# Which queue issues the loads and stores of the plain blocks, and five smaller moves, in an attention and two-layer kernel

## The chip, the core and the metric

The kernel runs on one core of a Trainium2 chip. The metric is the device time of one execution, in microseconds (us). PE is TensorE, DVE is VectorE, ACT is ScalarE, POOL is GpSimd, and SP is SyncE, which here does nothing but issue DMAs. DMAs can be issued from ACT too; each of the two has a queue of its own in the profile.

## What is computed

```python
# q, k, v: 8 x 8 x 576 x 64 (batch, heads, sequence, head width)
# attention inside chunks of 64 tokens:
scores = scale * matmul(q_c, k_c.T)
scores = scores - max(scores); attn = exp(scores); attn = attn / (sum(attn) + 1e-09)
x = matmul(attn, v_c), laid out as 4608 tokens x 512
# layer 1 (512 -> 1536 -> 512)
g = x @ w_gate; silu = g / (1 + exp(-g))
x = (silu * (x @ w_val)) @ w_out
# layer 2: the same on rows normed to unit mean square
xn = x / sqrt(mean(x * x) + 1e-6) * rms_g
out = (silu(xn @ w_gate2) * (xn @ w_val2)) @ w_out2
```

All is float32. The kernel splits each operand of a product into a high and a low half and runs three matmuls for each product (`mm3`, L642 to L645): high by high, low by high, high by low.

## The kernel before

The 4608 tokens are 36 tiles of 128 tokens. `home` (L321) gives the order in which they are worked on. The first 20 positions are five **plain blocks** of 512 tokens (`blocks`, j = 0 to 4), the list `last` (L320) names the 16 tiles behind them.

The plain blocks come first, up to about 614 us, in 60 iterations n, one for each block j and slice f of 128 columns of the 1536 (`NF` = 12). An iteration is 12 matmuls for g, 12 for v and 12 for y of the slice before, 36 in all. A list of steps (`put`, L806) is hung on it: after g, v and y of iteration n the steps 3n, 3n+1 and 3n+2 are run (`run`, in the main loop). In these steps the attention of the tiles 8 to 35 is done, one tile in about 4.5 steps: loads of q, k and v pieces (xq, xk, xv, issued through `issue`, L452), transposes on DVE (`trans_att`, L467 and L468), scores, softmax, the product with v (`att_pv`, whose result goes by `att_hi` into x of the block, or for the tail tiles through one x1 tile to memory, L607 to L613). The low halves of layer 1's weights are loaded from memory for every slice but a few, in `load_lo` (l, 512 KB) and `load_lo_o` (lo, 256 KB). Layer 2's weights are prepared beside this: loaded as w64, rebuilt, summed and stored as wsg or wsv in `comb_keep`. Layer 1's are summed for the later blocks by POOL (`whole`, L269 to L274, tiles wag, wav, wao of one tag with three buffers) and stored by SP.

Both queues issue in the order of the program. Up to iteration 19 SP issues all of it. From iteration 20 on ACT issues l and lo, right after its share of g; the stores of wsg and wsv (`comb_keep`) and the loads of w64 from the fourth on go to ACT over the whole of it. ACT also does casts (L242, L617, L675), the exponentials (L508) and the activations (L655), in one order with its issues.

Behind the plain blocks seven **large blocks** s = 0 to 6 follow, in seven products instead of eight (sums and differences of quarters). s = 0 and 1 are layer 1 of the 16 tail tiles; s = 2, 3, 4 (twice 512 tokens) and 5, 6 (twice 384) are layer 2. A large block has 84 steps for g and v (6 fp of 14 z), each of 6 matmuls at a spacing of 0.227 us (1.36 us a step), and then the y stage. Quarters of x (xf) are loaded in `x_load`, subtracted and split in `x_prep` (`sub` L1023 to L1027, `split`): for s = 0 by the table `XFIRST` in the last iterations of the plain blocks, later by `XNEXT` in the y stage. The norm of the large block before is done in the steps `extra`: sums of squares (`tail_sq`), cast and split (`tail_cast`, `tail_split`), a product with ones (`tail_mm`), root, multiply and store. In layer 2 the results are transposed into yo (`y_out`, L1204, two buffers per name) and stored by SP from a list, two or so at a time (`flush`, L1307); `rows` (L324) cuts the 512 or 384 tokens into runs that are consecutive in the output, and each run needs stores of its own.

The weights of the large blocks come through a ring of buffers (`load_ring`, L961 to L967), loaded by SP; those issues wait for the product that frees a buffer.

Of the kernel before, what the change touches and what calls it, by code (L numbers as in the profile page):

```python
# [9 lines left out]
F32 = mybir.dt.float32  # L10
# [9 lines left out]
def tile_kernel(  # L20
# [19 lines left out]
    nc = tc.nc  # L40
    B, H, S, D = q.shape
    NT, DM = out.shape
    DFF = moe_w_gate.shape[1]
    P = 128
# [205 lines left out]
    def comb_keep(nm, fp, k):  # L250
        z = SLOT[k]
        w = comb[1, nm, fp]["w", z // 2]
        a = z - z % 2
        queue = nc.sync if (nm, fp) in later2 else nc.scalar
        queue.dma_start(
            out=w2_d["gvo".index(nm), fp, :, a:z + 1], in_=w[:, :z - a + 1].bitcast(F32)
        )

    COMB = (
        (7, comb_add, 3), (7, comb_add, 4), (8, comb_add, 5), (8, comb_cast, 3), (8, comb_cast, 4),  # L260
        (9, comb_rest, 3), (9, comb_rest, 4), (11, comb_keep, 4), (10, comb_add, 6),
        (10, comb_cast, 0), (10, comb_cast, 5), (11, comb_rest, 0), (11, comb_rest, 5), (13, comb_keep, 5),
        (14, comb_cast, 1), (14, comb_cast, 6), (15, comb_rest, 1), (15, comb_rest, 6), (17, comb_keep, 6),
        (16, comb_cast, 2), (17, comb_rest, 2), (19, comb_keep, 2),
    )

    PLAIN = {"g": ((0, 0), (0, 1), (1, 1)), "v": ((0, 0), (0, 1), (1, 1)), "o": ((0, 0), (1, 0), (1, 1))}

    def whole(nm, j, p, side):  # L269
        f = 2 * p + side  # L270
        t = cv.tile([P, KD * P], F32, tag="wa", bufs=3, name=f"wa{nm}{f}")
        h = whi[0, nm, f]
        nc.gpsimd.tensor_add(t, h.bitcast(F32), low_of(0, j, chunk(j, f), nm).bitcast(F32))
        flat[0, nm, f] = t  # L274
# [42 lines left out]

    NCH = NT // CH
    SC = S // CH
    last = [12, 13, 14, 15, 20, 21, 22, 23, 28, 29, 30, 31, 32, 33, 34, 35]  # L320
    home = [i for i in range(NT // P) if i not in last] + last  # L321
    order = [home.index(i) for i in range(NT // P)]

# [283 lines left out]
    def att_hi(i, j):  # L607
        xb = xps[i]
        if j >= NB:
            t = att.tile([P, KD, P], F32, tag="x1", bufs=1, name=f"x1_{i}")  # L610
            nc.scalar.copy(t.rearrange("p h (c q) -> p c h q", c=2), xb)
            o = order[i] * P - TAIL
            nc.sync.dma_start(out=x1_d[:, o:o + P].rearrange("(h p) t -> p h t", p=P), in_=t)  # L613
            return
        xh, xl = x_tiles(0, j)
        o = order[i] * P - blocks[j][0]
        nc.scalar.copy(xh[:, :, o:o + P].rearrange("p h (c q) -> p c h q", c=2), xb)  # L617
# [270 lines left out]
    for x, (nm, f) in enumerate(w2):  # L888
        pos = NP + 8 * x
        if x == 0:  # L890
            put(0, 0, pos + 1, lambda nm=nm, f=f: load_w64(1, nm, f))
        put(0, 0, pos + 5, lambda nm=nm, f=f: rebase(1, nm, f))
        if x < 3:
            put(0, 0, pos + 8, lambda x=x: load_w64(1, *w2[x + 1]))
        elif x + 1 < len(w2):
            put(0, 0, pos + 6, lambda x=x: load_w64(1, *w2[x + 1], queue=nc.scalar))
        put(0, 0, pos + 7, lambda nm=nm, f=f: to_f32(1, nm, f))
        if f >= NP2:
            for d, fn, kk in COMB:
                put(0, 0, pos + 1 + d, lambda fn=fn, nm=nm, f=f, kk=kk: fn(nm, f - NP2, kk))  # L900

    for n in range(NF - 2, 20):
        if n >= NF:
            put(0, 0, 3 * n + 1, lambda n=n: load_lo_o(*iters[n], nc.sync))
        put(0, 0, 3 * n + 2, lambda n=n: load_lo(*iters[n + 2], nc.sync))

    w1_at = (
# [98 lines left out]
    def x_prep(s, kt):  # L1006
        tw = SB[s][1]

        def tiles(k):
            if (s, k) not in xo:  # L1010
                xo[s, k] = [
                    X2.tile(
                        [P, 1024 + (16 if (k, z) == (2, "l") else 0)], F32R, tag=f"xo{k}{z}", name=f"xo{k}{z}_{s}"
                    )[:, :1024].rearrange("p (a b) -> p a b", a=2)
                    for z in "hl"
                ]
            return xo[s, k]

        def split(k, nm):
            h, l = tiles(k)  # L1020
            x = xf[s, kt, nm]
            nc.scalar.copy(h[:, kt, :tw], x[:, :tw])
            nc.vector.tensor_sub(l[:, kt, :tw], x[:, :tw], h[:, kt, :tw].bitcast(F32))  # L1023

        def sub(o, a, b):
            o, a, b = (xf[s, kt, z][:, :tw] for z in (o, a, b))
            (nc.vector if s else nc.gpsimd).tensor_sub(o, a, b)  # L1027

        return {
            "0": lambda: split(0, "11"),  # L1030
            "A": lambda: sub("11", "12", "11"),
            "6": lambda: split(6, "22"),
            "B": lambda: sub("12", "22", "12"),
            "1": lambda: split(1, "21"),
            "C": lambda: sub("22", "22", "11"),
            "3": lambda: split(3, "11"),
            "D": lambda: sub("21", "21", "22"),
            "5": lambda: split(5, "12"),
            "4": lambda: split(4, "22"),
            "2": lambda: split(2, "21"),  # L1040
        }
# [345 lines left out]
    with tc.manual_schedule():  # L1387
# [22 lines left out]
        def conv1(z):  # L1410
# [67 lines left out]
        X2 = None  # L1478
        xops = {}
        XFIRST = {  # L1480
# [4 lines left out]
        }  # L1485
        XNEXT = {
# [6 lines left out]
        for n, (l, j, f) in enumerate(iters):  # L1493
# [31 lines left out]
            if prev is not None:  # L1525
                lo()
            sg, product = emit_g(l, j, f)
            if n >= 20 and n + 2 < len(iters):
                load_lo(*iters[n + 2], nc.scalar)
            if n >= 20:  # L1530
                load_lo_o(*iters[n], nc.scalar)
            run(0)
            if head:
                conv1(3 * f + 4 if f else 2)
# [45 lines left out]
        for s in range(NS):  # L1580
            norm = extra[s + 1]
            for z in range(2):
                for d in range(KD):
                    when(norm, 2 * d + 20 * z, tail_sq, s, z, d)
                when(norm, 8 + 20 * z, tail_cast, s, z)
                when(norm, 10 + 20 * z, tail_split, s, z)
                when(norm, 18 + 14 * z, tail_mm, s, z)
                when(norm, 34, tail_sqrt, s, z)
                when(norm, 36 + z, tail_mul, s, z)
                when(norm, 38 + 2 * z, tail_newton, s, z)  # L1590
            for n, (z, d) in enumerate(((0, 2), (0, 3), (1, 0), (1, 1), (0, 0), (0, 1), (1, 2), (1, 3))):
                when(norm, 42 + 2 * n, tail_x, s, z, d)
                when(norm, 44 + 2 * n, tail_keep, s, z, d)
        for s in range(len(SB)):
            for fp in range(NP2):
                banks = {}
                for z, (m, kk) in enumerate(GV):
                    gv_mm(s, fp, m, kk, banks)
                    wn += 1
                    if (s, fp, z) == (0, 0, 1):  # L1600
                        emit_y(*prev)
                        evac_y(*prev[:2])
                        one.close()
                        pairs.close()
                        psc = two.enter_context(
                            tc.tile_pool(name="psc", bufs=1, space=PSUM, reuse_waits="tile")
                        )
                        L2 = open_pool(two, "l2", 1, "left")
                        gv_after(s, fp, "g", 0, banks)
                        load_ring(wn + 15)  # L1610
                    if (s, fp, z) != (0, 0, 0):
                        gv_after(s, fp, m, kk, banks)
                        load_ring(wn + 16)
                        flush(z % 2)
                    for fn in extra.get(s, {}).get(14 * fp + z, ()):
                        fn()
                    ring_split(wn + 7)
                    if s + 1 < len(SB) and (fp, z) == (4, 4):
                        x_load(s + 1, 0)
                    if fp == NP2 - 1 and z >= 1 and z - 1 < 5:  # L1620
                        h_prep(s, z - 1)
                    if fp == NP2 - 1 and z in (7, 10, 11):
                        h_prep(s, z - 2 if z < 8 else z - 4)
                    if fp == 4 and z in (2, 6, 10):
                        h_t2(s, z // 4)
                    if fp == 5 and z in (2, 10):
                        h_t2(s, 3 + z // 8)
                h_t1(s, fp)
# [67 lines left out]
```

## Time and profile before

| | |
|---|---|
| time, median of 3 runs | 1764.28 us (1762.73 to 1767.71) |
| profiled execution: its time, its span | 1765.0 us, 1763.2 us |
| mean granted TensorE clock | 0.989 |
| busy: PE, DVE, ACT, POOL | 1702.8, 1193.8, 869.1, 524.7 us |
| DMA: SP's queue, ACT's queue | 361.49 MB, 42.61 MB |

A busy share is a mean over stages that differ: what a change in one stage is worth is read from that stage. Idle time counts where PE has it. The row of an instruction in a timeline ends with the idle time of its engine before it and with what ended it, in square brackets. A granted clock of 1.00 is 2.4 GHz, 0.50 is 1.2 GHz; a window between these holds both.

### The profile page before, as it was taken

How to read it: one execution, taken by the hardware profiler on the slowest of the kernel's cores; microseconds unless marked ns; L12 is line 12 of the kernel's file. 1: busy time of each engine (PE TensorE's matmuls, PEld its weight loads, DVE VectorE, ACT ScalarE, POOL GpSimd, SP SyncE). 2: the span in 40 equal slices, each digit the busy share in tenths (PEclk: the TensorE clock that was granted, in tenths of full speed). 3: DMA queues.
4: the chain of work that ended last, by engine and by line, in shares of the span. 5: the costliest groups of instructions: out<-in, count | busy, mean ns of one | idle time of the engine just before them, and what ended most of it. 6: DMA issues, size and time to landing. Idle time of an engine off the chain costs nothing.

```text
span 1763.2 us, 29688 instructions
## 1 busy us (share of the span) xinstructions
PE 1702.8 (97%) x9870; PEld 1434.5 (81%) x9870; DVE 1193.8 (68%) x1932; ACT 869.1 (49%) x2044; POOL 524.7 (30%) x517
## 2 busy tenths in 40 slices
PE   7999999898999999999999999999999999999998
PEld 5788777786778788877787888888888888999998
DVE  6996656665665578896889476933783477367456
ACT  6764544454444366665666355433542354344343
POOL 1004537565545256317742542000000000000000
PEclk9999999998999999999999999999999999999999
DMA  9997687977779668747785789887788778889786
GB/s 231 324 251 171 170 213 202 240 206 185 211 187 324 215 218 289 225 139 225 235 288 144 223 304 336 219 218 201 235 219 214 213 211 239 267 280 276 232 257 175
DMA packets 487063, 405.98 MB, mean 230 GB/s; under 512 B 279808, under 2 KB 363008, under 8 KB 486912
## 3 DMA queue, kind: packets, MB, share of 16 engines
q1 hardware_dynamic: 465328, 361.49, 71.3%
q10 hardware_dynamic: 21584, 42.61, 7.4%
q8 instruction: 79, 1.29, 0.3%
q14 instruction: 72, 0.59, 0.1%
HBM read 321.91 MB, written 82.05 MB: 229 GB/s over the span
## 4 chain that ended last, share of the span: by engine, by line
PE 75%; DMA 9%; DVE 8%; POOL 3%; ACT 2%; SPq 2%; issue 2%; ACTq 0%; DVEq 0%; POOLq 0%
PE g L645 2%; PE yvA L643 2%; PE ygA L643 2%; PE ygA L645 2%; PE yvA L645 2%; PE yvA L644 2%; PE ygA L644 2%; PE g L643 2%; PE g L644 2%; PE v L643 2%; DMA xk<-in_k_dram 2%; PE v L645 2%; PE v L644 2%; SPq L454 1%; DMA l<-lo_scratch 1%
## 5 line engine op out<-in xcount | busy, mean ns | idle before, releaser
L1128 POOL TENSOR_TENSOR h<-h,h 128x512 f32<-128x512 f32 (+1 forms) x42 | 56.9, 1355 | 674.4 <-DVE h L1106 673.8
L1164 DVE TENSOR_TENSOR hp<-h,hp 128x512 fp32r<-128x512 f32 (+1 forms) x252 | 164.9, 681 | 24.2 <-ACT hp L1163 19.5
L1087 ACT ACTIVATE sgt<-sgt 128x512 f32<-128x512 f32 (+1 forms) x126 | 76.2, 605 | 173.7 <-DVE sgt L1094 173.5
L1163 ACT CAST hp<-h 128x512 fp32r<-128x512 f32 (+1 forms) x252 | 141.5, 590 | 39.0 <-PE yvA L645 13.0
L536 POOL TENSOR_TENSOR p<-p,r 128x512 f32<-128x512 f32 x36 | 41.1, 1141 | 226.9 <-DVE r L535 168.1
L643 PE MATMUL v<-xh,wv 128*128 128x512 f32 x240 | 97.0, 404 | 3.1 <-DVE sg L672 2.0
L1106 DVE TENSOR_TENSOR h<-h,sgt 128x512 f32<-128x512 f32 (+1 forms) x126 | 88.6, 703 | 16.5 <-ACT sgt L1087 4.0
L643 PE MATMUL g<-xh,wg 128*128 128x512 f32 x240 | 95.7, 399 | 4.0 <-DVE sg L656 2.2
L645 PE MATMUL g<-xh,l 128*128 128x512 f32 x240 | 94.6, 394 | 3.4 <-DMA l<-lo_scratch 3.4
L645 PE MATMUL v<-xh,l 128*128 128x512 f32 x240 | 94.9, 395 | 0.0
L644 PE MATMUL g<-xl,wg 128*128 128x512 f32 x240 | 94.3, 393 | 0.3 <-DVE xl L637 0.3
L644 PE MATMUL v<-xl,wv 128*128 128x512 f32 x240 | 94.6, 394 | 0.0
L655 ACT ACTIVATE sg<-g 128x512 f32<-128x512 f32 x60 | 35.8, 597 | 80.4 <-PE g L645 70.4
L656 DVE SCALAR_TENSOR_TENSOR sg<-sg,g 128x512 f32<-128x512 f32 x60 | 40.9, 681 | 47.1 <-ACT sg L655 46.5
L675 ACT CAST hh<-sg 128x512 fp32r<-128x512 f32 x60 | 37.3, 621 | 70.1 <-DVE sg L672 65.1
L508 ACT ACTIVATE p<-both,m 128x64 f32<-128x64 f32 x224 | 67.1, 324 | 1.1
L644 PE MATMUL ygA<-hp,wro 128*128 128x512 f32 (+1 forms) x168 | 63.2, 376 | 0.5 <-DVE hp L1164 0.4
L643 PE MATMUL ygA<-hp,wro 128*128 128x512 f32 (+1 forms) x168 | 62.9, 375 | 0.4 <-ACT s3g L1080 0.4
L645 PE MATMUL ygA<-hp,wro 128*128 128x512 f32 (+1 forms) x168 | 62.8, 374 | 0.0
L643 PE MATMUL yvA<-hp,wro 128*128 128x512 f32 (+1 forms) x168 | 62.8, 374 | 0.0
L644 PE MATMUL yvA<-hp,wro 128*128 128x512 f32 (+1 forms) x168 | 62.7, 373 | 0.0
L645 PE MATMUL yvA<-hp,wro 128*128 128x512 f32 (+1 forms) x168 | 62.7, 373 | 0.0
(846 smaller groups left out, 5489.5 us busy)
## 6 DMA issues: line engine op xcount, KB each, us to landing
wrg<-w_scratch SPq DMA_DIRECT2D x210, 256.0 KB, 3.2
wrv<-w_scratch SPq DMA_DIRECT2D x210, 256.0 KB, 3.2
wro<-w_scratch SPq DMA_DIRECT2D x210, 256.0 KB, 3.3
l<-lo_scratch ACTq DMA_DIRECT2D x29, 512.0 KB, 4.9
wrg<-w_scratch SPq DMA_DIRECT2D x84, 128.0 KB, 2.9
wrv<-w_scratch SPq DMA_DIRECT2D x84, 128.0 KB, 3.1
wro<-w_scratch SPq DMA_DIRECT2D x84, 128.0 KB, 2.3
w_scratch<-wsg ACTq DMA_DIRECT2D x18, 512.0 KB, 3.9
```

The costliest lines, as they stand in the source:

```text
L508: nc.scalar.activation(pt[:, hp, x], s3[:, x, hp], AF.Exp, scale=SCALE, bias=m[:, x, hp:hp + 1], accum_out=r[:, 2 * hp + x],)
L536: nc.gpsimd.tensor_tensor(out=p8, in0=p8, in1=r.to_broadcast([P, HP * 2, CH]), op=ALU.mult)
L643: nc.tensor.matmul(o, sh, mh, start=first, stop=False, skip_group_check=free)
L644: nc.tensor.matmul(o, sh, ml, start=False, stop=False, skip_group_check=free)
L645: nc.tensor.matmul(o, sl, mh, start=False, stop=last, skip_group_check=free)
L656: return sg, lambda: nc.vector.scalar_tensor_tensor(out=sg[:, :n], in0=sg[:, :n], scalar=1.0, in1=g[:, :n], op0=ALU.add, op1=ALU.mult)
L675: nc.scalar.copy(hh[:, :n], sg[:, :n])
L1087: nc.scalar.activation(t[:, :tw], src[:, :tw], AF.Silu)
L1106: nc.vector.tensor_mul(h[:, :tw], src[:, :tw], sgt[pos][:, :tw])
L1128: nc.gpsimd.tensor_sub(a, a, b)
L1163: nc.scalar.copy(hh[:, :tw], src)
L1164: nc.vector.tensor_sub(hl[:, :tw], src, hh[:, :tw].bitcast(F32))
```

## The change

It has these parts.

1. Of the plain blocks' DMAs, those that ACT issued go to SP: `comb_keep`'s stores, one step later than before; w64 from the fourth on, two steps later; l and lo of iterations 20 and on, now steps of the list at 3n+1 (l of iteration n+2 and lo of n).
2. The tag of `whole`'s sums has four buffers, not three; x1 has two, not one.
3. `XFIRST` begins at step 29, not 26; three of its splits go to z = 2 and 4 of the first pass of s = 0 (`XREST`). Of its subtractions, those of kt = 1 go from POOL to DVE.
4. The tail norm: the second cast and split a step later, its product six steps later (38, not 32), all that follows six steps later; the first x quarters of the next large block are loaded ten steps later.
5. `last` holds tile 27 in place of 23, so that tile 23 is in the plain blocks and the tail's tiles are 12 to 15, 20 to 22, and 27 to 35.

```diff
     def comb_keep(nm, fp, k):
-        queue = nc.sync if (nm, fp) in later2 else nc.scalar
-        queue.dma_start(
+        nc.sync.dma_start(
             out=w2_d["gvo".index(nm), fp, :, a:z + 1], in_=w[:, :z - a + 1].bitcast(F32)
         )
     COMB = (
-        ... (11, comb_keep, 4) ... (13, comb_keep, 5) ... (17, comb_keep, 6) ... (19, comb_keep, 2),
+        ... (12, comb_keep, 4) ... (14, comb_keep, 5) ... (18, comb_keep, 6) ... (20, comb_keep, 2),
     def whole(nm, j, p, side):
-        t = cv.tile([P, KD * P], F32, tag="wa", bufs=3, name=f"wa{nm}{f}")
+        t = cv.tile([P, KD * P], F32, tag="wa", bufs=4, name=f"wa{nm}{f}")
-    last = [12, 13, 14, 15, 20, 21, 22, 23, 28, 29, 30, 31, 32, 33, 34, 35]
+    last = [12, 13, 14, 15, 20, 21, 22, 27, 28, 29, 30, 31, 32, 33, 34, 35]
     def att_hi(i, j):
-            t = att.tile([P, KD, P], F32, tag="x1", bufs=1, name=f"x1_{i}")
+            t = att.tile([P, KD, P], F32, tag="x1", bufs=2, name=f"x1_{i}")
-        if x < 3:
+        if x + 1 < len(w2):
             put(0, 0, pos + 8, lambda x=x: load_w64(1, *w2[x + 1]))
-        elif x + 1 < len(w2):
-            put(0, 0, pos + 6, lambda x=x: load_w64(1, *w2[x + 1], queue=nc.scalar))
-    for n in range(NF - 2, 20):
+    for n in range(NF - 2, len(iters)):
         if n >= NF:
             put(0, 0, 3 * n + 1, lambda n=n: load_lo_o(*iters[n], nc.sync))
-        put(0, 0, 3 * n + 2, lambda n=n: load_lo(*iters[n + 2], nc.sync))
+        if n + 2 < len(iters):
+            put(0, 0, 3 * n + (2 if n < 20 else 1), lambda n=n: load_lo(*iters[n + 2], nc.sync))
         def sub(o, a, b):
-            (nc.vector if s else nc.gpsimd).tensor_sub(o, a, b)
+            (nc.vector if s or kt else nc.gpsimd).tensor_sub(o, a, b)
         XFIRST = {
-            26: ((0, "0"),), 27: ((1, "0"), (0, "6"), (0, "A")), 28: ((1, "6"), (1, "A"), (0, "1")),
-            29: ((1, "1"), (0, "B")), 30: ((0, "3"), (1, "3"), (0, "C")), 31: ((0, "5"), (1, "B")),
-            32: ((1, "5"), (1, "C")), 33: ((0, "4"), (0, "D")), 34: ((1, "4"), (0, "2"), (1, "D")),
-            35: ((1, "2"),),
+            29: ((0, "0"), (1, "0"), (0, "A")), 30: ((0, "1"), (1, "1"), (0, "6"), (1, "A")),
+            31: ((0, "B"), (1, "6"), (1, "B")), 32: ((0, "C"), (1, "C"), (0, "3")), 33: ((0, "4"), (1, "3")),
+            34: ((1, "4"), (0, "D")), 35: ((0, "5"), (1, "D")),
         }
+        XREST = {2: ((1, "5"), (0, "2")), 4: ((1, "2"),)}
             sg, product = emit_g(l, j, f)
-            if n >= 20 and n + 2 < len(iters):
-                load_lo(*iters[n + 2], nc.scalar)
-            if n >= 20:
-                load_lo_o(*iters[n], nc.scalar)
-                when(norm, 8 + 20 * z, tail_cast, s, z)
-                when(norm, 10 + 20 * z, tail_split, s, z)
-                when(norm, 18 + 14 * z, tail_mm, s, z)
-                when(norm, 34, tail_sqrt, s, z)
+                when(norm, 8 + 21 * z, tail_cast, s, z)
+                when(norm, 10 + 21 * z, tail_split, s, z)
+                when(norm, 18 + 20 * z, tail_mm, s, z)
+                when(norm, 40, tail_sqrt, s, z)
...
-                when(norm, 42 + 2 * n, tail_x, s, z, d)
-                when(norm, 44 + 2 * n, tail_keep, s, z, d)
+                when(norm, 48 + 2 * n, tail_x, s, z, d)
+                when(norm, 50 + 2 * n, tail_keep, s, z, d)
+                    for kt, op in XREST.get(z, ()) if s + fp == 0 else ():
+                        xops[kt][op]()
-                    if s + 1 < len(SB) and (fp, z) == (4, 4):
+                    if s + 1 < len(SB) and (fp, z) == (5, 0):
                         x_load(s + 1, 0)
```

## Rows read from the trace of the kernel before

**Rows 1.** Waits of PE over the whole span: us in total, times, longest us.

```profile
PE ssq L752 <- POOL al L741: 7.8, 1, 7.8
PE both L482 <- DVE kT L467: 5.6, 1, 5.6
PE p0gA L643 <- ACT s2g L1080: 5.4, 1, 5.4
PE both L599 <- DVE pT L554: 5.0, 1, 5.0
...
PE tssq L1275 <- POOL ts L1267: 4.0, 1, 4.0
PE g L645 <- DMA l<-lo_scratch: 3.4, 2, 2.8
PE y L645 <- DMA lo<-lo_scratch: 3.1, 2, 1.7
...
PE v L643 <- DVE sg L672: 2.0, 1, 2.0
```

**Rows 2.** Windows of 5 us: busy us of each engine, granted clock, DMA share, GB/s.

```profile
345.00:350.00 5.00, 1.97 (x63) 1.85 (x63) 4.24 (x9) 1.12 (x2) 2.04 (x2) 0.59 0.75 202
...
600.00:605.00 5.00, 4.71 (x18) 3.47 (x16) 5.00 (x6) 1.66 (x3) 2.51 (x2) 0.81 0.80 258
...
840.00:845.00 5.00, 5.00 (x16) 3.95 (x16) 1.82 (x3) 2.71 (x6) 4.92 (x7) 0.66 0.11 30
...
1630.00:1635.00 5.00, 1.99 (x6) 1.99 (x7) 2.05 (x4) 1.27 (x3) 0.00 (x0) 0.77 0.03 6
```

**Rows 3.** Timeline of DVE, SP, POOL and ACT: start, us, instruction, idle before.

```profile
487.88 0.45 DVE L468 STREAM_TRANSPOSE qT<-xq 128x256 f32<-128x256 f32 x1 [9.79 <-DMA xk<-in_k_dram]
...
413.45 8.14 SPq L454 DMA_DIRECT2D xq<-in_q_dram  x4
...
433.52 1.26 POOL L273 TENSOR_TENSOR wao<-wo,lo 128x512 f32<-128x512 f32 x1 [15.05 <-DMA w_scratch<-wao]
...
278.81 0.59 ACT L611 COPY x<-both 128x512 f32<-128x512 f32 x1 [10.60 <-DMA x_scratch<-x]
```

**Rows 4.** Waits of SP's queue, 195 to 575 us.

```profile
SPq L454 <- DMA w_scratch<-wsg: 36.7, 10, 7.8
SPq L454 <- DMA l<-lo_scratch: 34.3, 12, 6.0
...
SPq L299 <- POOL wav L296: 4.2, 2, 3.0
```

**Rows 5.** Chain that ended last, 195 to 300 us: start, us, step.

```profile
201.54 2.62 DMA w_scratch<-wsg
...
204.54 0.46 SPq L454
```

**Rows 6.** DMA issues, 200 to 550 us (two rows), then 100 to 150 us (two rows).

```profile
l<-lo_scratch ACTq DMA_DIRECT2D x24, 512.0 KB, 4.7
...
w_scratch<-wv SPq DMA_DIRECT2D x3, 128.0 KB, 4.7
...
lo_scratch<-l SPq DMA_DIRECT2D x9, 256.0 KB, 3.9
...
xv<-in_v_dram SPq DMA_DIRECT2D x1, 256.0 KB, 3.6
```

**Rows 7.** A window of 50 us, with the columns of rows 2.

```profile
100.00:150.00 50.00, 49.71 (x341) 40.18 (x340) 38.29 (x60) 29.06 (x64) 3.75 (x3) 1.00 0.83 211
```

**Rows 8.** Timeline of POOL from 591 us.

```profile
591.04 11.47 POOL L1027 TENSOR_TENSOR xf<-xf,xf 128x512 f32<-128x512 f32 x7 [5.90 <-DVE xo0l L1023]
```

**Rows 9.** Line 1023 over the span: ns least/median/most, first and last start.

```profile
L1023 DVE TENSOR_TENSOR xo6l<-xf,xo6h x14: 547/679/1780, 590.9 to 1606.3; 128x512 fp32r<-128x512 f32 x10, 128x384 fp32r<-128x384 f32 x4
```

**Rows 10.** Timeline of POOL around 838 us.

```profile
837.96 1.78 POOL L1267 TENSOR_TENSOR ts<-tq,ts 128x512 fp32r<-128x512 f32 x1
```

**Rows 11.** Timeline of DVE at the end of large block 5.

```profile
1631.01 0.58 DVE L1204 STREAM_TRANSPOSE yo<-yt 128x384 f32<-128x384 f32 x1 [9.32 <-DMA out_dram<-yo]
```

More of the change, by code (lines that the diff above doesn't have):

```diff
@@ L260, in tile_kernel @@
         (7, comb_add, 3), (7, comb_add, 4), (8, comb_add, 5), (8, comb_cast, 3), (8, comb_cast, 4),
[L261 to L264, printed above, removed]
+        (9, comb_rest, 3), (9, comb_rest, 4), (12, comb_keep, 4), (10, comb_add, 6),
+        (10, comb_cast, 0), (10, comb_cast, 5), (11, comb_rest, 0), (11, comb_rest, 5), (14, comb_keep, 5),
+        (14, comb_cast, 1), (14, comb_cast, 6), (15, comb_rest, 1), (15, comb_rest, 6), (18, comb_keep, 6),
+        (16, comb_cast, 2), (17, comb_rest, 2), (20, comb_keep, 2),
     )
@@ L1584, in tile_kernel @@
                     when(norm, 2 * d + 20 * z, tail_sq, s, z, d)
-                when(norm, 8 + 20 * z, tail_cast, s, z)
-                when(norm, 10 + 20 * z, tail_split, s, z)
-                when(norm, 18 + 14 * z, tail_mm, s, z)
-                when(norm, 34, tail_sqrt, s, z)
-                when(norm, 36 + z, tail_mul, s, z)
-                when(norm, 38 + 2 * z, tail_newton, s, z)
+                when(norm, 8 + 21 * z, tail_cast, s, z)
+                when(norm, 10 + 21 * z, tail_split, s, z)
+                when(norm, 18 + 20 * z, tail_mm, s, z)
+                when(norm, 40, tail_sqrt, s, z)
+                when(norm, 42 + z, tail_mul, s, z)
+                when(norm, 44 + 2 * z, tail_newton, s, z)
             for n, (z, d) in enumerate(((0, 2), (0, 3), (1, 0), (1, 1), (0, 0), (0, 1), (1, 2), (1, 3))):
-                when(norm, 42 + 2 * n, tail_x, s, z, d)
-                when(norm, 44 + 2 * n, tail_keep, s, z, d)
+                when(norm, 48 + 2 * n, tail_x, s, z, d)
+                when(norm, 50 + 2 * n, tail_keep, s, z, d)
         for s in range(len(SB)):
```

## The prediction, made before the change was run

> **What bounds the kernel now.** I read the waits of TensorE (PE) first [rows 1]. PE is the bound, so a change can only pay by removing these waits, or the slow clock after them; the reader is to see that few waits carry the sum. Placed on the timeline, they are events: A, between 209 and 228 us, PE stands four times for l and lo, the low weight halves (3.4 + 3.1 = 6.5). B, around 280, about 2. C, at 343, 5.0 for pT of the attention. D, at 429, 7.8 for al of the norm. E, at 483, 5.6 for kT. F, 591 to 605, 2.9 in three pieces, the largest the 2.0 for sg. G, at 836, 4.0 for ts of the tail norm. H, at 1628, 5.4 at the last change of block.
>
> Next the windows of 5 us [rows 2]: after each stand the granted clock is lower for some 5 to 10 us. A window loses its PE busy time times what the clock lacks of 1: 1.97 x 0.41 = 0.8 in the first row. Up to 605 us eight windows are below 1, and between them they lose 7.7: C 2.2, D 2.3, E 1.9, F 1.3 (first and last of the eight stand there). Around 840 it is 5.00 x 0.34 = 1.7, and around 1630 it is 1.99 x 0.23 plus a remnant, 1.0. So with their clock A is 6.5, B 2.2, C 7.1, D 10.1, E 7.5, F 4.2, G 5.7, H 6.4: 49.7 us in all, and no version of this change can win much more.
>
> Then who is late. At E, VectorE (DVE) stood 9.79 us for xk before the transposes that PE wanted; at C it was the same with xq [rows 3]. xq and xk are loaded by SyncE (SP). The waits of SP's queue show it standing at xq/xk issues (L454) for landings that have nothing to do with them: 36.7 us for stores of wsg, 34.3 for loads of l [rows 4]. Both were issued by ScalarE (ACT). Where I followed them in the order of issue, the landing that ends such a stand is that of the eighth DMA before it, on either queue. The chain shows one: ACT came to its store of wsg at 201.54, it landed 2.62 us later, and only then SP went on with its xk issues [rows 5]. At 413.45 four xq issues took 8.14 us, for an l of ACT [rows 3]. So an ACT that is late with its issue stops SP, and through SP everything that SP loads. From 200 to 550 us 399 DMAs of SP and 87 of ACT were issued (27 groups; the first and the last stand in [rows 6]): 486 in 350 us, 0.72 us for each. PE's stands in that stretch, A to E, are 33.4, so without them the same 486 would have to go in 316.6 us, 0.65 each.
>
> **Stores and loads to SP.** All 87 (l, lo, the wsg and wsv stores, w64g and w64v) go to SP. Removed: SP's stands for a late ACT, 71 us in the two largest groups [rows 4], and ACT's own stands at such issues. Added: 87 issues on SP. An issue that waits for nothing takes 0.46 [rows 5], so 40 us. That is less than 71, and SP's pace should rise; how far, no row of this stretch shows. The bounds of the pace are 0.72, as today (nothing gained), and 50/86 = 0.58: from 100 to 150 us SP alone issued 86 DMAs (13 groups, the first and the last in [rows 6]) and PE was busy 49.71 of 50 us [rows 7]. At 0.58 the 486 take 283 us, and nothing is left of A, C and E; at 0.72 all of it is. The middle, 0.65, is just what PE needs. I take it, because the stretch carries larger transfers than 100 to 150 (24 l of 512 KB [rows 6] against none there) and its stores wait for computed tiles. A queue that just keeps pace on average is still late in bursts; I leave 10 of 21.1 us: **-11.1**, with ends 0 and -21.1. Where lo(n) now comes: step 3n+1, behind the attention loads of the step, for a product some 10 us later; l and lo take some 4.7 us to land [rows 6], so SP may lag by 5 us. That lag is what the 10 stands for. The stores of wsg come one step later (some 3 us); behind one that waits for POOL, every load of SP is queued.
>
> **The fourth wa buffer, and D.** POOL stood 15.05 us before a sum into wa for the landing of w_scratch<-wao [rows 3], and al, which PE wanted, was queued behind it. A fourth buffer moves the wait to the store before, a tile later; with an SP that is no longer late that store lands in time. **-9** of 10.1; if SP stays late, the buffer alone could still take it, or leave all of it: ends 0 and -10.1.
>
> **The second x1 buffer, and B.** ACT stood 10.60 us for the store of the single x1 tile [rows 3], and casts behind it reached PE late. Two buffers, with tails in turn several steps apart, remove it: **-2.2**.
>
> **Later x steps, and F.** From 591 us POOL ran seven x subtractions in 11.47 us [rows 8], and DVE's splits beside them took up to 1.78 us, against a median of 0.68 [rows 9]; PE then stood 2.0 for sg from DVE [rows 1]. The change gives four of the eight subtractions to DVE (0.68 each by L1023, the same shape: 2.7 us), starts three steps later, and moves three splits behind the block. ACT's stand of 2.7 us at its lo issue goes with the queue. The Trainium skill ("SBUF — State Buffer", the single rule on the shared port pair) says that a DVE instruction with two SBUF inputs and a GpSimd instruction that reads SBUF exclude each other for the whole instruction; 1.78 beside 0.68 agrees with that. By it the four moved ones cost DVE about what they blocked, so this edit alone is worth near nothing. My sum: four subtractions that each cost DVE 1.1 go, four of 0.68 come, 1.7 us net, three splits (2.0) go to after the block. DVE is ahead by some 3.7 against a stand of 2.9 in three places: **-3**, ends -4.2 and +3 (the same work in seven steps instead of ten, if DVE is late anyway). The three splits land at 620 us, where no PE wait of [rows 1] lies; with x_load ten steps later (13 us, still 19 us before its use), I put **+1** for both, ends 0 and 3.
>
> **Tail norm, and G.** ts left POOL at 837.96 + 1.78 = 839.7 [rows 10], 4.0 after PE wanted it [rows 1]. The product moves from step 32 to step 38, six steps of 1.36 us (six matmuls at a spacing of 0.227) = 8.2 us, the split by one step. 8.2 - 1.4 is more than 4.0. What follows (root, multiply, stores) moves by six steps too, within a block of 84; the load of the next block is moved behind it. **-5.7**; if POOL falls as far behind again, 0.
>
> **Tiles 23 and 27, and H.** DVE stood 9.32 us before a transpose into yo for the stores of the yo before [rows 11], and PE 5.4 for what came behind it. That block's tokens lie in two runs of the output, so each tile is stored in eight pieces, not four. With tile 27 among the last, all are single runs. Sixteen issues at 0.46 and their waits go. Other block ends have no such wait in [rows 1]: **-6.4**, end 0.
>
> **Sum.** -11.1 - 9 - 2.2 - 3 + 1 - 5.7 - 6.4 = -36.4 against the profiled execution, 1765.0: 1728.6. That execution is 0.7 above the median, so I say 1728.
>
> **Rivals.** *All goes* (1715): SP reaches the pace of 100 to 150, and A to H all vanish, -49.7. For it: the pace was seen. Against: the mix of transfers there was lighter.
> *The queue move nets nothing* (1740 to 1749): the landings, not who issues them, hold SP. A queue whose issue waits for the eighth landing before it goes no faster than eight landings allow, 4.7/8 = 0.59 us for each at the landing of l [rows 6], and any late store adds to that. The pace stays 0.72, and A, C and E stay, with xq late for SP's own stores. G, H, B, F and the cost give -16.3, 1748.7; with D's buffer, 1739.7. The Trainium skill ("DMA: Bandwidth & Descriptors", "Issuing engines are not separate DMA queues") says that all DMAs share the same engines whoever starts them and that more issuing engines save only issue time; by it the move brings 40 us more issue work to SP and takes nothing away. [rows 4] speak against that: SP stood 71 us for landings that were late because ACT issued them late.
> *Slower: SP stands at wsg stores for POOL* (1789). 24 wsg stores are now in SP's order. Today SP stood 3.0 us at the most for a POOL result, at a wav store [rows 4]. If it were 3.0 at each of the 24, 72 us come on top of 486 x 0.65 = 316: 388, 38 longer than today's 350. With G, H, F and the cost: 1765.0 - 14.1 + 38 = 1789. It makes the kernel slower by over 0.3% from 2.2 us per store on: (350 + 14.1 + 5.3 - 316)/24. Against: both such waits together were 4.2 us, and the stores now come a step later.
> *The change doesn't do what it says*: G or H returns by another path. Either costs about 6, the time becomes 1734, and that lies within the range.
>
> **How the numbers follow.** Forecast (1720 to 1737) 0.42, all goes (1710 to 1720) 0.20, the queue nets nothing (1737 to 1752) 0.24, slower by SP 0.07, something in between 0.07. The range 1710 to 1752 holds the first three, 0.86, and takes in the ends of every unknown price but F's and SP's worst. What a measurement can tell from no change is 0.3%, 5.3 us: faster 0.87, within 0.05, slower 0.08; G and H alone are more than that, and they do not depend on SP.
>
> **What would show it.** All DMAs of 0 to 620 us in SP's queue; SP's waits at L454 for wsg and l well below 71 us; PE's waits for l, lo, kT and pT together below 10 us; none for al, tssq, and p0gA at the last block. I am wrong if SP's waits for POOL at L255 exceed 20 us, or if PE's waits for lo grow beyond 10: then lo sits behind xq and xk.

## The result, and the profile after

| | before | changed |
|---|---|---|
| time, median | 1765.99 us (beside the later runs 1767 to 1768) | 1742.1 us (1741.62 to 1743.13) |
| ratio | | 0.9867, 95% interval 0.9848 to 0.9886 |
| profiled execution: time, span | 1765.0, 1763.2 | 1741.6, 1739.7 |
| granted clock | 0.989 | 0.994 |

The change makes the kernel some 23.5 us faster. 36.4 were forecast. The measured time lies in the stated range, where the rival in which the queue nets nothing had been put (1740 to 1749), though not by its way. The changed kernel measured once more, with the last four experiments, gave 1738.0 (ratio 0.983, interval 0.9816 to 0.9845). The two intervals of the same kernel do not meet, so between groups of runs a difference of some 7 us shows nothing.

The page first: PE's busy time, which was 1702.8, and the two queues. ACT's queue holds nothing but eight output stores at the end.

```profile
PE 1697.9 (98%) x9870; PEld 1431.4 (82%) x9870; DVE 1193.5 (69%) x1936; ACT 866.5 (50%) x2044; POOL 518.8 (30%) x513
...
q1 hardware_dynamic: 483456, 403.71, 80.1%
...
q10 hardware_dynamic: 3200, 0.39, 0.1%
```

The waits of PE in the changed kernel (us, times, longest), which answer to [rows 1]:

```profile
PE y L644 <- DMA lo<-lo_scratch: 20.6, 8, 3.8
PE qP L438 <- DMA tq<-in_q_dram: 4.2, 1, 4.2
PE s L481 <- ACT kT L447: 1.8, 2, 1.5
```

Every wait of [rows 1] but one is gone: al, kT, s2g, pT, ts, l and sg. In their place stands the one that had been the second smallest there, lo: 20.6 us for 3.1. (The wait for tq is at the very start and was there before.) Windows of 5 us say the same of the clock. Around 840 and 1630, where [rows 2] show 0.66 and 0.77, it is 1.00; after the waits for lo it is low in nine windows up to 595 us, two of which stand here, and these lose 6.9 us. (Two windows at 15 to 25 us, low in both kernels, are left out here as in the prediction.) In all, the eight events of the prediction (49.7 us) are gone, and one of 20.6 + 6.9 = 27.5 has come: -22.2, beside the measured -23.4 of the two profiled executions.

```profile
285.00:290.00 5.00, 4.92 (x16) 3.98 (x17) 0.83 (x3) 0.00 (x0) 3.95 (x5) 0.70 0.48 88
460.00:465.00 5.00, 2.95 (x7) 2.38 (x8) 0.75 (x2) 1.69 (x4) 0.00 (x0) 0.71 0.75 190
840.00:845.00 5.00, 5.00 (x24) 4.14 (x23) 4.41 (x5) 4.97 (x9) 4.65 (x4) 1.00 0.97 326
1630.00:1635.00 5.00, 5.00 (x31) 5.00 (x30) 2.23 (x4) 1.49 (x3) 1.01 (x1) 1.00 0.89 256
```

Then SP's waits from 195 to 575 us, which answer to [rows 4]. The 71 us for wsg and l have become 0.2 and 12.2. What is longest now is the store of x1 (L612), behind ACT's copy into it. Added up over all rows of this view, SP's stands for a landing fell from 135 to 23 us, and its stands for a result of another engine rose from 23 to 63.

```profile
SPq L612 <- ACT x L610: 26.7, 9, 6.4
SPq L453 <- DMA l<-lo_scratch: 12.2, 12, 2.6
SPq L298 <- POOL wav L295: 6.9, 3, 3.7
...
SPq L453 <- DMA w_scratch<-wsg: 0.2, 1, 0.2
```

And the timeline of SP ahead of the first long wait for lo (lo of iteration 26, wanted in iteration 27), with PE's row behind it. PE came for lo at 285.08 - 3.80 = 281.28. In these rows SP issues almost without a pause, half a microsecond each; lo stands behind the q and k pieces and comes to be issued at 279.97, 1.3 us before it is wanted, and PE goes on 5.1 us after that issue.

```profile
276.95 1.44 SPq L453 DMA_DIRECT2D xq<-in_q_dram  x3
278.44 0.94 SPq L453 DMA_DIRECT2D xk<-in_k_dram  x2
279.48 0.40 SPq L254 DMA_DIRECT2D w_scratch<-wsg  x1
279.97 1.08 SPq L204 DMA_DIRECT2D lo<-lo_scratch  x1
```
```profile
285.08 0.79 PE L644 MATMUL y<-hh,lo 128*128 128x512 f32 x1 [3.80 <-DMA lo<-lo_scratch]
```

### The profile page after: what moved, and what is told of

The parts are those of the page before. It is cut to its first block, busy times and chain, and to the rows that moved or that the text cites. A ratio compares the mean times of both kernels' runs of the same rounds, so it can differ in the third digit from the quotient of the medians.

```text
span 1739.7 us, 29674 instructions
## 1 busy us (share of the span) xinstructions
PE 1697.9 (98%) x9870; PEld 1431.4 (82%) x9870; DVE 1193.5 (69%) x1936; ACT 866.5 (50%) x2044; POOL 518.8 (30%) x513
## 3 DMA queue, kind: packets, MB, share of 16 engines
q1 hardware_dynamic: 483456, 403.71, 80.1%
## 4 chain that ended last, share of the span: by engine, by line
PE 80%; DVE 7%; DMA 6%; SPq 3%; issue 1%; POOL 1%; ACT 1%; DVEq 0%; POOLq 0%; ACTq 0%
PE g L642 2%; PE g L644 2%; PE g L643 2%; PE v L642 2%; PE v L643 2%; PE v L644 2%; SPq L453 2%; PE yvA L644 2%; PE yvA L642 2%; PE ygA L642 2%; PE ygA L644 2%; PE ygA L643 2%; PE yvA L643 2%; DMA lo<-lo_scratch 2%; DMA l<-lo_scratch 1%
## 5 line engine op out<-in xcount | busy, mean ns | idle before, releaser
L644 PE MATMUL y<-hh,lo 128*128 128x512 f32 x120 | 49.3, 411 | 20.6 <-DMA lo<-lo_scratch 20.6
L671 DVE SCALAR_TENSOR_TENSOR sg<-v,sg 128x512 f32<-128x512 f32 x60 | 41.0, 684 | 35.0 <-PE v L644 34.3
L643 PE MATMUL ygA<-hp,wro 128*128 128x512 f32 (+1 forms) x168 | 63.2, 376 | 0.5 <-DVE hp L1162 0.4
L642 PE MATMUL ygA<-hp,wro 128*128 128x512 f32 (+1 forms) x168 | 63.0, 375 | 0.5 <-ACT s3g L1078 0.5
L642 PE MATMUL yvA<-hp,wro 128*128 128x512 f32 (+1 forms) x168 | 62.7, 373 | 0.0
L643 PE MATMUL yvA<-hp,wro 128*128 128x512 f32 (+1 forms) x168 | 62.7, 373 | 0.0
```

What stands on the lines that cost most here:

```text
L642: nc.tensor.matmul(o, sh, mh, start=first, stop=False, skip_group_check=free)
L643: nc.tensor.matmul(o, sh, ml, start=False, stop=False, skip_group_check=free)
L644: nc.tensor.matmul(o, sl, mh, start=False, stop=last, skip_group_check=free)
L671: nc.vector.scalar_tensor_tensor(out=sg[:, :n], in0=vv[:, :n], scalar=0.5, in1=sg[:, :n], op0=ALU.mult, op1=ALU.mult)
```

## The experiments

Two theories at the outset. Q: SP is now late by the time of its own issues, in bursts, and lo, which is asked for one iteration ahead only, is what lands late. B: the transfers are too slow, and lo is late because the DMA engines are full. All ratios are to runs of the kernel before on the same chip; the experiments ran in three groups, and times of two groups are compared by these ratios.

### The queue move alone, and all the rest alone

The first is the kernel before with part 1 only; the second is the changed kernel with part 1 undone.

> The kernel before with only the move of the plain blocks' loads and stores to SP (with their new steps). Theory Q (each of SP's issues takes about 0.5 us, and in bursts SP falls behind its list; lo, one iteration ahead, is what then lands late): waits of PE for lo of about 20 us as in the changed kernel, none for kT or pT above 1 us, G (ts, 4.0) and H (s2g, 5.4) as before; 1754 to 1760. D (al) tells what the fourth wa buffer was for: if the queue alone takes the wait away, al is below 1 us and the time is at the lower end; if the buffer was needed, al is 5 to 8 us and the time 1762 to 1770. Rival R (the gain came from the smaller moves, the queue trades one wait for another): 1764 or more.

> The changed kernel with the queue move undone (ACT issues l, lo, wsg, w64 as before), all other parts kept. Theory Q: G and H gone (-12.1), B and F gone or halved (-3 to -6), A, C and E still there (20 us); D gone if the fourth buffer takes it, else 10 more: 1738 to 1751, and SP's waits at L453 for wsg and l still 60 us or more. Rival R: as fast as the changed kernel or faster, 1735 to 1742, with PE's waits for l, lo, kT and pT together at 20 us.

Measured: the queue move alone 1743.2 us (ratio 0.987, interval 0.985 to 0.989), the rest alone 1753.7 (0.9914, 0.989 to 0.9939). PE's waits in the first:

```profile
PE y L644 <- DMA lo<-lo_scratch: 18.6, 9, 4.7
PE p0gA L642 <- ACT s2g L1078: 5.5, 1, 5.5
...
PE tssq L1273 <- POOL ts L1265: 4.0, 1, 4.0
```

and in the second:

```profile
PE both L482 <- DVE kT L468: 6.1, 2, 5.0
PE both L482 <- DVE kT L467: 5.8, 1, 5.8
...
PE g L645 <- DMA l<-lo_scratch: 5.0, 1, 5.0
...
PE both L599 <- DVE pT L554: 4.0, 1, 4.0
```

SP's waits from 195 to 575 us in the second:

```profile
SPq L454 <- DMA l<-lo_scratch: 39.3, 12, 5.3
SPq L454 <- DMA w_scratch<-wsg: 29.0, 10, 7.3
```

The queue move alone takes away the waits of A to F that stood there before, but for lo: no al, no kT, no pT, no l, no sg, with three wa buffers and one x1 tile. G and H stand as before. The rest alone takes G and H, and al too; but SP is as late as before (68 us in the two rows, where it was 71), and a new wait for kT (5.0, at 447 us) has come where al's went. Its gain, 13.8 us, is G and H (12.1) and little else. The waits came in the main as theory Q had them, both times did not: I expected 1754 to 1760 of the first, which gave less, and at most 1751 of the second, which gave more. The two gains add to 24.3 + 13.8 = 38.1, and together they give 23.5 (30 by the ratio of the repeat). A wait that both take away, al, can explain no more than the 1.7 us that the second gains beside G and H. So something in the rest costs 6 to 13 us, once the queue has moved.

### lo earlier

```diff
-            put(0, 0, 3 * n + 1, lambda n=n: load_lo_o(*iters[n], nc.sync))
+            put(0, 0, 3 * n + (1 if n < 20 else -1), lambda n=n: load_lo_o(*iters[n], nc.sync))
```

> The changed kernel with lo of iteration n issued at step 3n-1, not 3n+1 (from n = 20 on), two steps or some 6 us earlier. In the changed kernel lo is issued 11 to 16 us after the start of its iteration where PE waits, and lands up to 5 us late. Theory Q: PE's waits for lo fall from 20.6 us to below 4, nothing takes their place, and the time is 1714 to 1722. Rival B (the transfers themselves are too slow, the DMA engines are full): lo's wait becomes one for l, kT or pT of the same size, 1736 to 1742.

1729.1 us (0.9787, 0.9768 to 0.9805). Waits of PE:

```profile
PE g L644 <- DMA l<-lo_scratch: 6.6, 4, 3.3
...
PE y L644 <- DMA lo<-lo_scratch: 0.8, 1, 0.8
```

lo is off the path, and a third of its wait has gone to l, which now stands behind it in the same list. The time lies between the two expectations; SP is still late, only for another load. By itself this run does not decide between Q and B, since an earlier issue helps a slow transfer too.

### Half as many q and k pieces

```diff
-        for hp in range(HP):
+        for hp in range(0, HP, 2):
...
-                            t[32 * z:32 * z + 32, hp, 2 * o:2 * (o + m), :],
...
+                            tf[32 * z:32 * z + 32, a:a + n, :],
+                            rw[b, r:r + 32 * n, 32 * e:32 * e + 32].rearrange("(tb p) i -> p tb i", p=32),
```

> The changed kernel with the q and k pieces of the attention in half as many DMAs, each of twice the size and a little over (32 issues per group become 16; bytes and packets of the same size, up to an eighth more). The pieces are read from other tokens, so the attention of the tiles 8 to 35 works on wrong q and k; all else is computed as it is. Theory Q: SP has 8 us more per group, lo is issued 4 to 8 us after the start of its iteration, PE's waits for lo fall below 4 us: 1713 to 1720. Rival B: the bytes are the same, so lo lands as late as before, waits of 15 to 20 us and 1737 to 1743.

1721.7 us (0.9743, 0.9726 to 0.976). SP's queue moved 404.61 MB, against 403.71, and PE's wait for lo fell to

```profile
PE y L645 <- DMA lo<-lo_scratch: 8.7, 5, 5.3
```

of which 5.3 is one wait at 563 us, behind the loads of the ring, where no q and k pieces are left. (Below 4 us and at most 1720 had been expected.) The bytes are the same, lo takes as long to land (4.3 us against 4.5, medians of 200 to 550 us), and all but 3.4 us of the wait among the pieces is gone: it was the number of issues ahead of lo, not the transfers. This decides for Q against B. With each issue go half a microsecond and, at times, a stand for an earlier landing (23 us in the changed kernel from 195 to 575 us, 8 here); the run does not part these two.

### Tile 23 back, and the x1 stores later

The first is the changed kernel with part 5 undone. In the second the store waits for two more steps:

```diff
-            nc.sync.dma_start(out=x1_d[:, o:o + P].rearrange("(h p) t -> p h t", p=P), in_=t)
+            x1s.append([2, x1_d[:, o:o + P].rearrange("(h p) t -> p h t", p=P), t])
...
+                x1_store()
```

> The changed kernel with tile 23 back among the last and 27 in the plain blocks (part 5 undone), all else kept. Theory S (with tile 27 among the last its x1 store comes in iteration 43, where SP stood 5.4 us for ACT before it and two groups of q and k pieces are due; PE then waited for lo in iterations 41 and 45): H comes back (s2g 5 to 6 us and its clock, 6 to 8 in all), the waits for lo after iteration 41 fall by 5 to 8 us, and the time stays within 3 us of the changed kernel, 1739 to 1745. Rival T (the tile has no part in the waits for lo, and the queue move alone merely had a lucky course): H comes back and nothing goes, 1746 to 1751.

> The changed kernel with the stores of x1 (the attention results of the last tiles) issued two steps, some 6 us, later in SP's list. In the changed kernel SP stood 26.7 us in nine of them for ACT's copy, with every load behind it. Theory S (a head of line that waits makes SP late, and with it lo): SP's waits at the x1 store for ACT fall below 5 us, PE's waits for lo from 20.6 to 8 to 14 us, 1728 to 1736. Theory Q alone (SP is late by the time of its issues, the stands at the stores lie where it is ahead): 1738 to 1743.

Measured: tile 23 back 1740.8 us (0.9847, 0.9831 to 0.9863), so the same as the changed kernel; the x1 stores later 1728.2 (0.9778, 0.9758 to 0.9797). Waits of PE with tile 23 back:

```profile
PE y L644 <- DMA lo<-lo_scratch: 16.4, 8, 4.5
PE p0gA L642 <- ACT s2g L1078: 5.9, 1, 5.9
```

H is back, with 2.2 us of clock, 8.1 in all, and the time is the same: the waits for lo are 4.2 us less, and the slow clock behind them costs 4.1 less. (Behind iteration 41 these waits fell from 11.3 to 8.4, by less than the 5 to 8 that were expected.) Counted from one first matmul for g to the next, iteration 45 took 14.3 us in the changed kernel, 14.8 when it was run again and 13.4 without parts 2 and 3 (below); it took 9.48 with tile 23 back, and 9.48 with the queue move alone. The timeline of SP in the changed kernel shows why:

```profile
435.62 0.41 SPq L254 DMA_DIRECT2D w_scratch<-wsg  x1
441.46 0.39 SPq L612 DMA_DIRECT2D x_scratch<-x  x1
441.94 2.64 SPq L453 DMA_DIRECT2D xk<-in_k_dram  x4
```

From 436.03 to 441.46 SP stood for the store of tile 27's x1, with the pieces of two groups and lo behind it; with tile 23 among the last that x1 store comes some six iterations earlier (four tiles of 4.5 steps). The iterations 41 to 47 together took 74.0, 72.5 and 74.5 us in the three kernels with tile 27 among the last, 67.3 and 69.3 in the two with tile 23. With the stores issued two steps later, and tile 27 still among the last, they took 68.4, and iteration 45 took 9.48: the late store was the cause. PE's wait for lo and SP's for ACT in that kernel:

```profile
PE y L653 <- DMA lo<-lo_scratch: 10.5, 6, 2.3
```
```profile
SPq L612 <- ACT x L619: 4.5, 2, 4.3
```

26.7 us of stands have become 4.5; 10 us of PE's wait for lo are gone, and 2.2 of the 6.9 of its clock. So the lag has two sources: SP's issues, and its stands at the x1 stores. They are not a sum. With half as many pieces SP stood even longer at these stores, 6.3 us of it at that of tile 27, and iteration 45 took 9.57 us all the same:

```profile
SPq L613 <- ACT x L611: 41.8, 11, 6.4
```

So a stand at these stores costs PE only where the issues behind it fill the time that is left.

### Both early, and the small parts undone

The first puts lo and l at step 3n-1 and the x1 stores two steps later; the second is the changed kernel without parts 2 and 3; the third is the first with the fourth wa buffer and the move of the x steps undone.

```diff
-            put(0, 0, 3 * n + (2 if n < 20 else 1), lambda n=n: load_lo(*iters[n + 2], nc.sync))
+            put(0, 0, 3 * n + (2 if n < 20 else -1), lambda n=n: load_lo(*iters[n + 2], nc.sync))
```

> The changed kernel with lo of iteration n and l of iteration n+2 both issued at step 3n-1 (from n = 20 on) and the x1 stores two steps later. lo alone at that step gave 1729 and left waits for l of 6.6 us. If both theories hold, l and lo are off the path: PE's waits for l and lo together below 4 us, 1716 to 1724. If SP's issue time is what lacks, the waits go to kT or pT of the attention, whose loads now stand behind them: 5 us or more there, 1726 to 1732.

> The changed kernel with the fourth wa buffer, the second x1 buffer and the move of the x steps undone (parts 2 and 3), the queue move, the tail norm and tile 27 kept. With the queue move alone no wait for al, none of ACT for the x1 tile and none for sg was left, though none of these parts was in it. So I expect no difference from the changed kernel: 1739 to 1745, al and sg below 1 us. Rival (they are needed once tile 27 and the rest change the order): 1747 or more, with al (5 us or more) or sg (2 us or more) among PE's waits.

> The version with lo and l early and the x1 stores later (1720), with the fourth wa buffer and the move of the x steps undone. If these two parts are worth nothing once SP is in time: 1716 to 1723, al and sg below 1.5 us among PE's waits. If they matter there: 1725 or more, with al or sg of 3 us or more.

Both early: **1719.5 us** (0.9725, 0.9709 to 0.9742), the fastest of all runs, 2.75% below before, as expected if both theories hold; kT and pT together are below 2 us. Its longest waits of PE behind the start:

```profile
PE y L653 <- DMA lo<-lo_scratch: 2.3, 1, 2.3
...
PE g L651 <- DVE sg L664: 1.2, 2, 0.7
```

Without parts 2 and 3: 1737.4 us (0.9823, 0.9805 to 0.9841), not slower than the changed kernel run again (1738.0, 0.983). No al and no sg is among its waits, as expected; it has

```profile
PE y L644 <- DMA lo<-lo_scratch: 17.1, 8, 3.9
```

In the third, without the fourth buffer and the move of the x steps, it is 1724.6 (0.9754, 0.9739 to 0.9769), between the two expectations, with

```profile
PE g L651 <- DVE sg L664: 2.6, 3, 1.1
```

That is 5 us more than both early with these parts. The two ran in different groups, and the intervals of their ratios overlap by 0.0003, so it stays open what these parts are worth there.

### lo alone on ACT

```diff
             sg, product = emit_g(l, j, f)
+            if n >= 20:
+                load_lo_o(*iters[n], nc.scalar)
             run(0)
```

> The changed kernel with lo alone (from iteration 20 on) issued by ACT again, right after its share of g, all the rest on SP: 38 issues fewer on SP, and lo no longer behind the q and k pieces. If another issuing engine only saves issue time and otherwise costs nothing, lo is in time and nothing else changes: 1716 to 1724, SP's waits for landings of lo below 5 us. Theory L (SP's issues wait for the eighth landing before them, so SP stands wherever ACT issues late): SP's waits at L453 for landings of lo 15 us or more, waits of PE for lo, kT or pT of 10 us or more, 1728 to 1745.

1772.9 us (1.0032, 1.0017 to 1.0047): 0.3% slower than before, with 34 loads (not 38) moved from SP to ACT and nothing else. PE's wait, SP's waits, and two steps of the chain:

```profile
PE g L644 <- DMA l<-lo_scratch: 39.0, 13, 6.0
```
```profile
SPq L453 <- DMA lo<-lo_scratch: 44.2, 14, 6.0
...
SPq L298 <- DMA lo<-lo_scratch: 15.1, 4, 7.4
SPq L612 <- DMA lo<-lo_scratch: 6.7, 2, 3.6
SPq L254 <- DMA lo<-lo_scratch: 6.4, 1, 6.4
```
```profile
400.86 2.60 DMA lo<-lo_scratch
403.47 0.31 SPq L453
```

SP stood 72 us for landings of lo, of which none of its own DMAs has any need. ACT came to this lo at 400.86; it landed at 403.46, and SP, which had issued nothing since 398.5, went on at 403.47. It is [rows 5] again, made by this one edit. Theory L had the stands; its bound for the harm, 1745, was too low by 28 us, and PE's wait came for l, which SP issues, and not for lo, kT or pT. The trace also shows why it is the eighth landing: the DMAs of both queues carry eight semaphores by turns (260 DMAs each), and every stand of SP for a landing from 195 to 575 us, 43 here, 73 in the kernel before, ends with the DMA that had the semaphore of the one SP is about to issue. The Trainium skill ("DMA: Bandwidth & Descriptors", "Issuing engines are not separate DMA queues") has more issuing engines save issue time; here the measurement decides, and a second engine, with 34 issues of 0.33 us, cost 35 us against the changed kernel that ran beside it.

### The buffers alone, and the changed kernel again

> The kernel before with part 2 only: four wa buffers, two x1 buffers. The prediction gave these D and B, -11.2: 1753 to 1757 beside a median of 1766 to 1768. The rival that the runs so far suggest (al and the x1 tile were late because SP was late; the buffers take those two waits away, and the late SP shows at the next place, kT or pT): al below 1 us, but PE's waits for kT, pT, l and lo together 25 us or more, and 1760 to 1768.

> The changed kernel once more, on the same chip as its variants: 1740 to 1745, waits for lo of 17 to 23 us. If it comes out at 1737 or less, the gain of the version without parts 2 and 3 (1737) was a difference of chips.

The kernel before with part 2 only: 1764.4 us (0.9982, 0.9967 to 0.9997). al is not among its waits, the time is the rival's and not the 1753 to 1757 of the prediction, but

```profile
PE both L482 <- DVE kT L467: 5.7, 1, 5.7
...
PE both L482 <- DVE kT L468: 4.0, 2, 3.0
PE both L599 <- DVE pT L554: 3.9, 1, 3.9
```

are: kT has gone from 5.6 to 9.7, and one of its three waits is new, at 445.5 us, behind a load of xk that SP issued only at 443.49 and that landed 4.4 us later:

```profile
448.04 0.45 DVE L468 STREAM_TRANSPOSE kT<-xk 128x256 f32<-128x256 f32 x1 [3.57 <-DMA xk<-in_k_dram]
```

The fourth buffer takes most of POOL's stand, and the late SP shows one group of tiles later. kT, pT, l and lo together are 19.3 us, not the 25 that the rival had asked for (17.1 before).

The changed kernel again: 1738.0 us, below the 1740 to 1745 that were expected, and one above the bound at which the gain of the version without parts 2 and 3 was to count as a difference of chips; the ratios (0.983 and 0.9823) show no difference. Its waits for lo are 17.7 us in 11 places, where they were 20.6 in eight, and the slow clock costs 2.8 us and not 6.9, which accounts for its lead over the first measurement.

## Why the prediction came out as it did

The sign and the range held; the sum was 13 us too good (10 by the repeat). Two of its own signs of being wrong came true: the waits for l, lo, kT and pT together are 20.6 us and not below 10, and those for lo alone exceed 10.

**A, C, E and lo.** This is the term that was mis-sized. I left 10 us of A, C and E for the lag of SP. All 21.1 went, and 27.5 came: 20.6 us of waits for lo and 6.9 of slow clock behind them (17.7 and 2.8 in the repeat). The failing step is the sentence that SP may lag by 5 us. It did not ask how far it lags in a burst. The pace I worked with was a mean: 0.65 us for each DMA, and in the changed kernel it is 350/500 = 0.70 over 200 to 550 us. Neither this nor the 0.58 of 100 to 150 us is what SP can do: SP also stands for landings and for results, 86 us from 195 to 575, and is late where its issues come close together. The experiments give the two things it left out. Issues follow each other at half a microsecond, with 8 or more q and k pieces between lo and the step before (halving their number: -15 to -22 us, against the repeat and the first measurement). And an SP that is in time stands at stores of data that are not there yet: I priced this for the stores of wsg behind POOL, where it was 1.2 us, and not for the x1 stores behind ACT, where it was 26.7 (two steps later: -9 to -16 us). The trace before had that wait already, in the fourth row of the view of [rows 4]:

```profile
SPq L613 <- ACT x L611: 12.2, 3, 7.0
```

The sign of the lag was in the text, though as a way to be wrong: lo beyond 10 us, behind xq and xk.

**D and B.** Gone, as forecast, but the 11.2 us were not the buffers' to give, so this part of the sum came right by luck. The queue move alone took both; the buffers alone took al's wait too, and gave 0.2% of time. The 15.05 us of POOL for w_scratch<-wao [rows 3] was a store that SP issued late: the sums had left POOL at 411.2 us, SP then needed 8.14 us for four xq issues, for an l of ACT, and came to the store at 429.68.

```profile
429.68 0.86 SPq L299 DMA_DIRECT2D w_scratch<-wao  x2
```

The prediction read the wait as a lack of buffers, and named SP's lateness only as a condition.

**F.** Gone with the queue move alone, in which POOL still runs all eight subtractions. There too DVE's splits take up to 1774 ns beside them, as this row of line 1021 shows (ns least/median/most), and PE waits for no sg. But PE's waits for lo stand at the same place there (1.8 and 4.7 us at 567 and 577), and may hide a wait for sg.

```profile
L1021 DVE TENSOR_TENSOR xo1l<-xf,xo1h x14: 545/682/1774, 569.8 to 1589.1; 128x512 fp32r<-128x512 f32 x10, 128x384 fp32r<-128x384 f32 x4
```

So the rule of the Trainium skill that I weighed there ("SBUF — State Buffer", the single rule on the shared port pair) agrees with the splits in the kernel before and with the queue move alone (1.78 and 1.77 beside 0.68 us). How much of F it made is not shown. In the version with lo early and parts 2 and 3 undone but for the x1 buffer, where no wait for lo hides them, PE's waits beside POOL's subtractions are 1.6 us (0.9 for hl, 0.7 for sg), where they were 2.9; with these parts there is none. What is left of the 2.9 may be ACT's stand at its issue (2.7 us), which was not tried by itself. In the changed kernel a wait for lo stands at that place too (2.7 and 3.7 us at 573 and 584).

**G and H.** Both gone, with their clock, as forecast, and present whenever their part was left out (4.0 and 5.5 with the queue move alone, 5.9 for H with tile 23 back). What the sum missed is that part 5 moves an x1 store as well as sixteen output stores. The order of the tiles decides where SP stands, and with an SP at its limit that cost 3 to 7 us in iterations 41 to 47, of the 8.1 that H gave.

**The rivals.** That all goes (1715) needed lo earlier and the x1 stores later, and then came within 5 us: 1719.5. That the queue move nets nothing has fallen: alone it is worth 24 us. The rival on the slow side had the right mechanism, a store at the head of SP's list that waits for an engine, at the wrong store: 26.7 us in nine of them, where 72 in 24 had been asked for.

What stays open: why the slow clock follows some waits for lo and not others (three of the eight show none), what made PE stand in F, and what parts 2 and 3 are worth once SP is in time.

## What to carry to other kernels

When loads and stores move to one in-order queue, do not price them by a mean pace: write down, for each load that has little lead, how many issues and which waiting stores stand between it and the step before, at the issue time that the trace shows. Before loads go to a second queue, look whose landings the first one's issues wait for. Where a wait for a buffer ends with a store, look when that store was issued: here it was late, and another buffer only moved the wait. When the order of tiles is changed for one stage, look for every DMA that goes with a tile, in all stages.

## What the runs showed of the hardware

I had not expected a second issuing queue to cost so much where it is late: 34 loads of 256 KB on ACT's queue, which took 0.33 us each to issue, made SP stand 72 us, and the kernel was 35 us slower than the changed kernel beside it. What ties the two queues in these traces are the eight semaphores that their DMAs share. That is how this program gives them out; whether queues that share none would hold each other up, no run here shows.
